# Early weight loads, freed slots and other DMA queues in an attention and GLU kernel

## Chip, cores and metric

The kernel runs on one core of a Trainium2 chip. The metric is the time of one execution on the device in microseconds (us), as the median of several runs. Profiles show one execution; their times count from the span's start. Engines are named as in the profile: PE is TensorE, PEld its weight load, DVE VectorE, ACT ScalarE, POOL GpSimd, SP SyncE. A name with q (SPq, ACTq, POOLq) is the engine's part that issues DMAs.

## What is computed

A pre-norm transformer layer in float32 on x of 2048 rows by 576 columns:

```python
x = A_x
h = x + _A_ref(_layernorm(x), A_wqkv, A_wo)      # 32 heads of 18; 8 keys, 2 positions apart
h2 = h + _B_ref(_layernorm(h), B_w_gate, B_w_up, B_w_down)
# _A_ref: logits = q . k at pos - 2*w (w = 0..7), softmax, weighted v, times wo
# _B_ref: (sigmoid(x @ w_gate) * (x @ w_up)) @ w_down, inner width 4608
```

## The kernel before

Even and odd positions are independent in the attention, so the rows are cut into four blocks of 512: blocks 0 and 1 are the even ones, 2 and 3 the odd ones. A block is held as four tiles (j) of 128 rows. Float32 operands of a product are split into a rounded high part and the remainder: `split` (L103) is one copy on ACT that rounds and one subtraction on DVE; each product is then three matmuls (high by high, low by high, high by low). The 576 columns are four chunks of 128 and a rest of 64; `split_rest` (L107) packs the rest's high and low part into one chunk.

*First stage.* `load_x(b)` (L331) reads a block by four DMAs on SP. `ln1` (L338) normalizes it tile by tile: `ln_j` (L118) takes statistics on DVE, the power on POOL and, for block 0, the scale on DVE (L134) and a copy of the rest columns (L135); PE transposes the tile (L139, L143) and `split` makes th and tl from it. `raw_w` and `qkv_w` (L355, L365) load and split the weights of a group of eight heads; `qkv` (L377) projects a block for one group and stores q, k and v to DRAM. `att_all` (L399) is a generator of attention steps, nearly all DVE work, that is stepped between projections. Blocks 0 and 1 come first; `front` (L478) multiplies block 0's attention output by wo, adds x, normalizes again and makes the first operands X of the GLU; it stores the transposed result to DRAM from a tile of the tag tok (L505, x<-tok in the profile). Near the end item 0's GLU weights are loaded into a slot of the tag tl (L538) and split by `first_split` (L507) into a slot of the tag th.

*Second stage.* The pools of the first stage are closed and their memory is used for new ones (gw, gh, gd, gc, st). Each new tile waits for the last users of the bytes under it. The 4608 inner columns are 36 chunks. An item is one chunk for one pair of blocks: kind std for one block (28 matmuls of 512 columns, `single` L644) or pair for two blocks with seven products instead of eight (`pair` L673). Items 0 to 13 are std for block 0, 14 to 35 are pair for blocks 0 and 1, then the same for blocks 2 and 3. For each item `load_gu` (L563) loads the weights into one of two buffers wg on SP, and `weights` (L575) splits them into w1 (two buffers), w2, w3, w4 and d; this is done one item ahead. Item 1's load goes out on POOL instead (L979), and item 0's down weights are split into a d tile of the new pool (L980, L981). The down product runs a pair of chunks behind (`down_tile`, L714, dp in the profile).

*Under the items* runs a second thread (`under_first` L888, `under_rest` L907), stepped by `bg_step` between matmul groups: the rest of block 1's attention, then `proj_scr` (L818), which does for block 1 what `front` did for block 0, and `operands`, which makes what pair items need. During the later items the same is done for blocks 2 and 3. `proj_scr` reads the attention output back from DRAM (`load_j` with i = 0, oj in the profile), the split wo half (wow), and x (`load_j` with i = 1, hj). All these loads are `paced` (L568): issued on SP behind the newest weight load.

*Order.* A scheduler puts every engine's instructions in one fixed order when the program is built: by trace order, moved forward by `tc.high_priority(n)` (HI is 400, HC 700), each as soon as it thinks the operands ready. `tc.issue_after(i)` puts instructions of the same engine behind i in that order, without a wait. On the chip each engine, and each DMA-issuing queue, works through its order and waits at its head.

Of the kernel before, what the change touches and what calls it, by code (L numbers as in the profile page):

```python
# [21 lines left out]
P = 128  # L22
# [38 lines left out]
def kernel(ctx, tc, x, wqkv, wo, wmlp, out):  # L61
# [36 lines left out]
    def f32(ap):  # L98
        return ap.bitcast(F32)
# [1 line left out]
    splits = []  # L101

    def split(hi, lo, src):  # L103
        act.activation(hi, src, AF.Copy)  # L104
        splits.append(dve.tensor_tensor(lo, src, f32(hi), ALU.subtract))  # L105

    def split_rest(t, src):  # L107
        act.activation(t, src, AF.Copy)
# [9 lines left out]
    def ln_j(xj, xn, on_act):  # L118
        bs = sm.tile([P, 2, 6], F32, bufs=4, name="bs")
        mv = sm.tile([P, 2], F32, bufs=4, name="mv")  # L120
        rstd = sm.tile([P, 1], F32, bufs=4, name="rstd")
        for k in range(2):
            dve.bn_stats(bs[:, k], xj[:, k * DH2:(k + 1) * DH2])
        dve.bn_aggr(mv, bs)
        dve.tensor_scalar(rstd, mv[:, 1:2], EPS, None, ALU.add)
        pool.tensor_tensor(rstd, rstd, mhalf, ALU.pow)
        if on_act:
            nm = sm.tile([P, 1], F32, bufs=4, name="nm")
            dve.tensor_scalar(nm, mv[:, 0:1], -1.0, None, ALU.mult)
            act.activation(xn[:, :D], xj, AF.Identity, bias=nm)  # L130
            act.activation(xn[:, :D], xn[:, :D], AF.Copy, scale=rstd)
            act.activation(xn[:, D:DX], xn[:, DM:D], AF.Copy)
        else:
            dve.tensor_scalar(xn[:, :D], xj, mv[:, 0:1], rstd, ALU.subtract, ALU.mult)  # L134
            dve.tensor_copy(xn[:, D:DX], xn[:, DM:D])  # L135

    def tr_main(ps, xn):
        for c in range(4):
# [86 lines left out]
    def step(gen, n):  # L225
        for _ in range(n):
            if next(gen, END) is END:
                return

    def drain(gen):  # L230
        for _ in gen:
            pass

    def run(*gens):
        live = list(gens)
        while live:
            live = [gn for gn in live if next(gn, END) is not END]
# [90 lines left out]
    def ev_tile(shape):  # L328
        return sar.tile(shape, F32, tag="ev", bufs=2, name="ev")

    def load_x(b):  # L331
        e, hf = BLOCKS[b]
        t = sah.tile([P, NS, D], F32, bufs=2, name="h")
        for j in range(NS):
            sp.dma_start(t[:, j], xv[e, hf][:, j])
        return t

    def ln1(b, xb):  # L338
        th = th3_tile(F32R) if b == 3 else th_tile()
        tl = tl_tile()  # L340
        yield th, tl
        xn = tok_tile()
        for j in range(NS):
            js = slice(j * P, (j + 1) * P)
            pri = 2 * HI if b == 0 else HI if b > 1 else 0
            with tc.high_priority(pri):
                ln_j(xb[:, j], xn[:, j], b > 1)
            pv = tr_main(mm_tile(), xn[:, j])
            pr = tr_rest(acc_tile(), xn[:, j])
            with tc.high_priority(pri):  # L350
                split(th[:, 0:4, js], tl[:, :, js], pv)
                split_rest(th[:, 4, js], pr)
            yield

    def raw_w(g):  # L355
        if g == 3:
            wr = sah.tile([P, NS, D], F32, bufs=2, name="h").rearrange("p j d -> p (j d)")
            wr = wr[:, :QC].rearrange("p (c n) -> p c n", c=5)
        else:
            wr = swo.tile([P, 5, NQ], F32, tag="wo", name="wr")  # L360
        for c in range(5):
            sp.dma_start(wr[:, c], wqkv[g][:, c * NQ:(c + 1) * NQ])
        return wr

    def qkv_w(g, wr=None):  # L365
        w = saw.tile([P, 2, 5, NQ], F32R, tag="qw", bufs=2, name="qw")
        for c in range(5):
            if wr is None:
                ws = sas.tile([P, NQ], F32, tag="wst", bufs=3, name="ws")
                sp.dma_start(ws, wqkv[g][:, c * NQ:(c + 1) * NQ])  # L370
            else:
                ws = wr[:, c]
            with tc.high_priority(3 * HI if g == 0 else HI):
                split(w[:, 0, c], w[:, 1, c], ws)
        return w

    def qkv(b, g, T, w):  # L377
        e, hf = BLOCKS[b]
        ev = ev_tile([P, 3, NS, CG])
        for j in range(NS):  # L380
            ps = acc_tile()
            passes.append(tok_major(ps, NQ, *T, slice(j * P, (j + 1) * P), w[:, 0], w[:, 1]))
            with tc.high_priority(HI):
                act.activation(ev[:, :, j], ps[:, :NQ].rearrange("p (t c) -> p t c", t=3), AF.Copy)  # L384
            yield
        r0 = LP + hf * TB
        with tc.high_priority(HI):
            act.dma_start(qscr[b][g], ev[:, 0].rearrange("p j c -> p (j c)"))
            for t, s in ((1, kscr), (2, vscr)):
# [173 lines left out]
    def load_gu(f, eng=sp, n=WC):  # L563
        ws = gw.tile([P, WC], F32, bufs=2, name="wg")
        behind[0] = eng.dma_start(ws[:, :n], wmlp[f][:, :n])
        return ws

    def paced(dst, src):  # L568
        with tc.issue_after(getattr(behind[0], "ins", behind[0])):
            behind[0] = sp.dma_start(dst, src)  # L570

    def d_tile():
        return gd.tile([P, 2, D], F32R, bufs=4, name="d")
# [235 lines left out]
            paced(f32(ww[a]), wscr[1][:, a])  # L809
        return tuple(ww)  # L810

    def load_j(pj, b, j, i):
        e, hf = BLOCKS[b]
        t = pj.tile([P, D if i else DX], F32, bufs=NS, name="hj" if i else "oj")
        paced(t, (xv[e, hf] if i else oscr[b])[:, j])
        return t

    def proj_scr(pj, b, raw, wos, ins=None, after=None):  # L818
        e, hf = BLOCKS[b]
        th, tl = th_tile(), tl_tile()  # L820

        def tile_j(t, j):
            js = slice(j * P, (j + 1) * P)

            def put(pv, cs):
                if cs.start == 0:
                    if b < 2:
                        pool.dma_start(hacc[b][:, j], t[1])
                    else:
                        rows = slice(0, 7, 6) if b == 2 else slice(2, 5, 2)  # L830
                        pool.dma_start(hsev[:, j // 2, rows, j % 2],
                                       t[1].rearrange("p (i n) -> p i n", i=2))
                act.activation(raw[:, cs, js], pv, AF.Copy)

            yield from proj_j(bg_bank, t, wos, th[:, :, js], tl[:, :, js], lambda: t[0], put, (1, 0))

        todo = []
        if ins is None:
            ins = []
            for j in range(NS):  # L840
# [24 lines left out]
        if b == 1:  # L865
            act.dma_start(xscr[b], raw[:, 0:2])
        return nxt
# [242 lines left out]
    for c, (kind, p, f) in enumerate(items):  # L1110
# [11 lines left out]
        if c == NF + NSTD:  # L1122
# [105 lines left out]
```

## Time and profile before

| | |
|---|---|
| median of 3 runs | 1590.44 us (1589.95 to 1590.81) |
| span of the profiled execution | 1589.2 us |
| PE, DVE, ACT, POOL busy | 98%, 80%, 55%, 12% |
| granted TensorE clock, mean | 0.993 |
| HBM read and written | 145.88 MB, 128.52 MB |

The profiled execution has no time of its own beside its span. In a group or timeline row stand the line, engine and operation, written and read tile, shapes, and in brackets how long the engine was idle before it and what ended that. A wait row reads: waiter, what it waited for, us in total, times, longest. The chain of waits is followed back from the last instruction. A busy PE can be a slow one: the granted clock is given with the windows.

### The profile page before, as it was taken

How to read it: one execution, taken by the hardware profiler on the slowest of the kernel's cores; microseconds unless marked ns; L12 is line 12 of the kernel's file. 1: busy time of each engine (PE TensorE's matmuls, PEld its weight loads, DVE VectorE, ACT ScalarE, POOL GpSimd, SP SyncE). 2: the span in 40 equal slices, each digit the busy share in tenths (PEclk: the TensorE clock that was granted, in tenths of full speed). 3: DMA queues.
4: the chain of work that ended last, by engine and by line, in shares of the span. 5: the costliest groups of instructions: out<-in, count | busy, mean ns of one | idle time of the engine just before them, and what ended most of it. 6: DMA issues, size and time to landing. Idle time of an engine off the chain costs nothing.

```text
span 1589.2 us, 22383 instructions
## 1 busy us (share of the span) xinstructions
PE 1553.3 (98%) x8532; PEld 1381.6 (87%) x8532; DVE 1268.1 (80%) x1931; ACT 869.2 (55%) x1546; POOL 184.2 (12%) x230
## 2 busy tenths in 40 slices
PE   7999979999999999999989999999999999999998
PEld 6999968888888888888879988888888888888887
DVE  7999988959999999999546687876677776677755
ACT  4432234425555666656443255776677776677761
POOL 1000000011010001000101100122112112212210
PEclk9999999999999999999999999999999999999999
DMA  7664544346367565665764234899989999989983
GB/s 267 208 206 163 193 184 165 133 177 246 104 164 205 157 170 139 166 191 149 210 203 143 100 110 110 182 186 181 176 169 183 184 173 180 177 170 182 184 170 124
DMA packets 76892, 273.50 MB, mean 172 GB/s; under 512 B 8336, under 2 KB 14224, under 8 KB 75888
## 3 DMA queue, kind: packets, MB, share of 16 engines
q0 software_dynamic: 27792, 105.89, 36.3%
q1 hardware_dynamic: 41360, 146.06, 27.4%
q10 hardware_dynamic: 7632, 20.12, 3.3%
q8 instruction: 67, 1.10, 0.3%
q14 instruction: 41, 0.34, 0.1%
HBM read 145.88 MB, written 128.52 MB: 173 GB/s over the span
## 4 chain that ended last, share of the span: by engine, by line
PE 55%; issue 27%; POOL 7%; DVE 6%; DMA 4%; ACT 1%; SPq 0%; POOLq 0%; ACTq 0%; DVEq 0%
PE b L609 23%; PE dp L723 15%; POOL h L794 7%; PE acc L150 6%; PE b L616 4%; PE b L150 1%; PE bgp L150 1%; DMA wg<-in_wmlp_dram 1%; DVE pr L182 1%; DMA x<-tok 1%; DVE pr L208 1%; DVE lg L186 1%; PE acc L152 1%; DMA tail<-h 1%; PE acc L153 1%
## 5 line engine op out<-in xcount | busy, mean ns | idle before, releaser
L609 PE MATMUL b<-tl,w 128*128 128x512 f32 x1716 | 438.1, 395 | 9.1 <-ACT w L104 6.5
L609 PEld LDWEIGHTS b<-tl,w 128*128 128x128 f32 x1716 | 311.7, 189 | 66.5 <-ACT w L104 7.7
L609 PE MATMUL b<-th,w 128*128 128x512 f32 x1368 | 352.8, 393 | 0.4 <-DVE s L698 0.3
L609 PEld LDWEIGHTS b<-th,w 128*128 128x128 f32 x1368 | 249.8, 188 | 46.7 <-DVE s L698 0.7
L104 ACT ACTIVATE w<-wg 128x640 fp32r<-128x640 f32 (+2 forms) x197 | 117.0, 598 | 125.2 <-PE b L616 59.8
L791 ACT ACTIVATE ev<-dp 128x576 f32<-128x576 f32 x224 | 145.0, 647 | 61.8 <-PE dp L785 58.2
L616 PE MATMUL b<-th,w 128*128 128x512 f32 x572 | 177.0, 391 | 0.0
L794 POOL DMA_DIRECT2D h<-ev x128 | 110.2, 862 | 456.8 <-ACT ev L791 440.5
L105 DVE TENSOR_TENSOR w<-wg,w 128x640 fp32r<-128x640 f32 (+2 forms) x197 | 126.8, 649 | 38.7 <-ACT w L104 38.3
L150 PE MATMUL acc<-qw,th 128*128 128x432 f32 x512 | 155.7, 365 | 1.2 <-DVE th L109 0.9
L105 DVE TENSOR_TENSOR w<-tw,w 128x512 fp32r<-128x512 f32 x116 | 79.6, 687 | 81.1 <-ACT w L104 80.2
L616 PEld LDWEIGHTS b<-th,w 128*128 128x128 f32 x572 | 107.7, 188 | 23.1
L723 PE MATMUL dp<-d,h0h 128*128 128x288 f32 x640 | 119.0, 296 | 1.7 <-DVE tail L733 1.7
L723 PE MATMUL dp<-d,h1h 128*128 128x288 f32 x640 | 120.0, 297 | 0.0
L723 PEld LDWEIGHTS dp<-d,h0h 128*128 128x128 f32 x640 | 99.4, 189 | 5.5 <-DVE tail L733 2.0
L150 PEld LDWEIGHTS acc<-qw,th 128*128 128x128 f32 x512 | 97.2, 190 | 6.5 <-DVE th L109 1.1
L723 PEld LDWEIGHTS dp<-d,h1h 128*128 128x128 f32 x640 | 99.5, 190 | 2.9
L731 ACT ACTIVATE stage<-dp 128x576 f32<-128x576 f32 x96 | 61.7, 646 | 62.4 <-PE dp L723 62.3
L104 ACT ACTIVATE w<-tw 128x512 fp32r<-128x512 f32 x116 | 72.8, 628 | 41.3 <-PE b L609 40.9
L150 PE MATMUL acc<-qw,tl 128*128 128x432 f32 x256 | 92.8, 362 | 0.0
L384 ACT ACTIVATE ev<-acc 128x432 f32<-128x432 f32 x64 | 33.9, 531 | 104.4 <-PE acc L153 97.7
L182 DVE TENSOR_TENSOR pr<-kw,q 128x2304 f32<-128x2304 f32 x32 | 81.7, 2552 | 2.8 <-DMA kw<-k 2.6
(278 smaller groups left out, 2899.8 us busy)
## 6 DMA issues: line engine op xcount, KB each, us to landing
h<-ev POOLq DMA_DIRECT2D x96, 576.0 KB, 7.2
wg<-in_wmlp_dram SPq DMA_DIRECT2D x49, 928.0 KB, 5.2
h<-stage POOLq DMA_DIRECT2D x24, 1152.0 KB, 10.6
wg<-in_wmlp_dram SPq DMA_DIRECT2D x36, 640.0 KB, 4.1
kw<-k SPq DMA_DIRECT2D x16, 792.0 KB, 4.4
vw<-v SPq DMA_DIRECT2D x16, 792.0 KB, 5.5
wd<-in_wmlp_dram SPq DMA_DIRECT2D x18, 576.0 KB, 7.2
h<-ev POOLq DMA_DIRECT2D x32, 288.0 KB, 6.8
```

The source lines that it names most:

```text
L104: act.activation(hi, src, AF.Copy)
L105: splits.append(dve.tensor_tensor(lo, src, f32(hi), ALU.subtract))
L150: pe.matmul(ps[:, :n], a[:, c, js], m[:, c], start=k == 0, stop=False)
L152: pe.matmul(ps[:, :n], th[:, 4, js], wh[:, 4], start=False, stop=False)
L182: dve.tensor_tensor(pr, both(kw, u), q[:, us].unsqueeze(2).broadcast_to([P, 2, W, CG]), ALU.mult)
L384: act.activation(ev[:, :, j], ps[:, :NQ].rearrange("p (t c) -> p t c", t=3), AF.Copy)
L609: pe.matmul(ps, wt[:, a, k0 + c], xx[:, m + c], start=first and k == 0, stop=k == 5, skip_group_check=True)
L616: pe.matmul(ps, wt[:, a, k0], xx[:, 4], start=False, stop=a == 1, skip_group_check=True)
L723: pe.matmul(ps[:, i, :DH2], a[:, js], d[:, m, i * DH2:(i + 1) * DH2], start=k == 0, stop=k == n)
L731: act.activation(hv, ps, AF.Copy)
L791: act.activation(hs[:, k % 2], ps[:, :, :DH2], AF.Copy)
L794: pool.dma_start(hsev[:, u, k0:k + 1], hs[:, :k + 1 - k0], accum_op=ALU.add, max_dma_last_dim=8 * D)
```

## The change

At the start, row tile 0 of block 0 is loaded first, then the first group's weights, then the other three tiles. The norm of tile 0 gets a higher priority. The norm of tile 1 is put behind the end of tile 0's norm on DVE, those of tiles 2 and 3 behind tile 0's split. The weight splits of the first group are put behind tile 0's norm (chunk 0) or split (chunks 1 to 4), those of the second group behind tile 0's split.

At the step to the GLU, item 1's weights are read on SP into the slot of the tag h in the first stage's pool, under the priority HI, after the projection of block 1 for the last group. Both first items' down weights and item 1's gate and up weights are split into slots of the tags tl and th, which live through both stages. The block that loaded item 1 on POOL and split item 0's down weights into a d tile is gone.

In `proj_scr`, block 1's oj loads go out on POOL and block 2's oj, wow and hj loads on ACT, neither paced. Block 1's wow and hj stay paced on SP, and so do block 3's loads.

```diff
@@ split
-        act.activation(hi, src, AF.Copy)
+        first = act.activation(hi, src, AF.Copy)
         splits.append(dve.tensor_tensor(lo, src, f32(hi), ALU.subtract))
+        return first, splits[-1]
@@ ln1
+            pri = (2 if j else 4) * HI if b == 0 else HI if b > 1 else 0
+            with ExitStack() as way:
+                way.enter_context(tc.high_priority(pri))
+                if b == 0 and j:
+                    way.enter_context(behind_all(done[j - 1:j] if j == 1 else cut[0][1:]))
+                done.append(ln_j(xb[:, j], xn[:, j], b > 1))
...
+                cut[j:] = [split(th[:, 0:4, js], tl[:, :, js], pv)]
@@ qkv_w
-            with tc.high_priority(3 * HI if g == 0 else HI):
+            with tc.high_priority(3 * HI if g == 0 else HI), behind_all(ties[c]):
@@ first stage
-    xb = load_x(0)
-    w = [qkv_w(0, raw_w(0))]
-    gl = ln1(0, xb)
+    xb = load_x(0, (0,))
+    wr = raw_w(0)
+    load_x(0, range(1, NS), xb)
+    normed, cut = [], []
+    gl = ln1(0, xb, normed, cut)
     T.append(next(gl))
-    run(gl, qkv(0, 0, T[0], w[0]))
-    w.append(qkv_w(1))
+    next(gl)
+    w = [qkv_w(0, wr, [normed[:1]] + [cut[0][1:]] * 2 + [cut[0]] * 2)]
+    call = qkv(0, 0, T[0], w[0])
+    next(call)
+    run(gl, call)
+    w.append(qkv_w(1, None, [cut[0]] * 5))
...
+    with tc.high_priority(HI):
+        wg1 = sah.tile([P, NS, D], F32, bufs=2, name="h").rearrange("p j d -> p (j d)")[:, :WC]
+        sp.dma_start(wg1, wmlp[1])
...
+    def first_down(ws):
+        d = xt.tile([P, 2, D], F32R, tag="tl", bufs=4, name="df")
+        split(d[:, 0], d[:, 1], ws[:, GU:WC])
+        return d
+
+    with tc.high_priority(HI):
+        wc = ww, first_down(wg)
+        wc_next = first_split(wg1), first_down(wg1)
@@ load_j, proj_scr
+        if eng is None:
+            paced(t, src)
+        else:
+            eng.dma_start(t, src)
...
-                ins.append([load_j(pj, b, j, 0), None])
+                ins.append([load_j(pj, b, j, 0, pool if b == 1 else act), None])
...
-            paced(f32(ww), wscr[0])
+            if b == 1:
+                paced(f32(ww), wscr[0])
+            else:
+                act.dma_start(f32(ww), wscr[0])
...
-                    ins[j][1] = load_j(pj, b, j, 1)
+                    ins[j][1] = load_j(pj, b, j, 1, None if b == 1 else act)
@@ items
-    with tc.high_priority(2 * HI):
-        wg2 = load_gu(1, pool)
-        d = d_tile()
-        split(d[:, 0], d[:, 1], wg[:, GU:WC])
-        wc = ww, d
-    wg = wg2
...
-        if c + 1 < len(items):
+        if c == 0:
+            wc = wc_next
+        elif c + 1 < len(items):
             wc = weights(items[c + 1][0], wg, c + 1 < NF + NSTD)
```

`behind_all(ties)` enters `tc.issue_after` for each instruction in ties.

More of the change, by code (lines that the diff above doesn't have):

```diff
@@ L134, in ln_j @@
             dve.tensor_scalar(xn[:, :D], xj, mv[:, 0:1], rstd, ALU.subtract, ALU.mult)
-            dve.tensor_copy(xn[:, D:DX], xn[:, DM:D])
+            return dve.tensor_copy(xn[:, D:DX], xn[:, DM:D])
     def tr_main(ps, xn):
@@ L329, in ev_tile, with behind_all, load_x, ln1 @@
         return sar.tile(shape, F32, tag="ev", bufs=2, name="ev")
-    def load_x(b):
+    def behind_all(ties):
+        way = ExitStack()
+        for i in ties:
+            way.enter_context(tc.issue_after(getattr(i, "ins", i)))
+        return way
+    def load_x(b, js=range(NS), t=None):
         e, hf = BLOCKS[b]
-        t = sah.tile([P, NS, D], F32, bufs=2, name="h")
-        for j in range(NS):
+        if t is None:
+            t = sah.tile([P, NS, D], F32, bufs=2, name="h")
+        for j in js:
             sp.dma_start(t[:, j], xv[e, hf][:, j])
         return t
-    def ln1(b, xb):
+    def ln1(b, xb, done=None, cut=None):
+        done = [] if done is None else done
+        cut = [] if cut is None else cut
         th = th3_tile(F32R) if b == 3 else th_tile()
@@ L344, in ln1 @@
             js = slice(j * P, (j + 1) * P)
-            pri = 2 * HI if b == 0 else HI if b > 1 else 0
-            with tc.high_priority(pri):
-                ln_j(xb[:, j], xn[:, j], b > 1)
+            pri = (2 if j else 4) * HI if b == 0 else HI if b > 1 else 0
[4 more added lines that the diff above has]
+                done.append(ln_j(xb[:, j], xn[:, j], b > 1))
             pv = tr_main(mm_tile(), xn[:, j])
@@ L350, in ln1 @@
             with tc.high_priority(pri):
-                split(th[:, 0:4, js], tl[:, :, js], pv)
+                cut[j:] = [split(th[:, 0:4, js], tl[:, :, js], pv)]
                 split_rest(th[:, 4, js], pr)
@@ L363, in raw_w, with qkv_w @@
         return wr
-    def qkv_w(g, wr=None):
+    def qkv_w(g, wr=None, ties=((),) * 5):
         w = saw.tile([P, 2, 5, NQ], F32R, tag="qw", bufs=2, name="qw")
@@ L810, in wos_early, with load_j @@
         return tuple(ww)
-    def load_j(pj, b, j, i):
+    def load_j(pj, b, j, i, eng=None):
         e, hf = BLOCKS[b]
         t = pj.tile([P, D if i else DX], F32, bufs=NS, name="hj" if i else "oj")
-        paced(t, (xv[e, hf] if i else oscr[b])[:, j])
+        src = (xv[e, hf] if i else oscr[b])[:, j]
+        if eng is None:
+            paced(t, src)
+        else:
+            eng.dma_start(t, src)
         return t
```

## Prediction

> **What bounds the kernel now.** I read the page first, then TensorE's waits stretch by stretch, then the windows around them.
>
> ```profile
> span 1589.2 us, 22383 instructions
> PE 1553.3 (98%) x8532; PEld 1381.6 (87%) x8532; DVE 1268.1 (80%) x1931; ACT 869.2 (55%) x1546; POOL 184.2 (12%) x230
> ```
>
> TensorE is busy for 98% of the span, so 35.9 us idle, and slow matmuls around the idle stretches, are all that an edit of order can win. The waits of PE are few:
>
> ```profile
> PE mm L139 <- DVE tok L134: 9.1, 1, 9.1
> PE acc L143 <- DVE tok L135: 1.6, 1, 1.6
> PE b L609 <- ACT w L104: 6.5, 1, 6.5
> PE b L609 <- DVE s L629: 2.5, 1, 2.5
> PE b L139 <- DMA oj<-o: 2.4, 1, 2.4
> PE bgp L139 <- DVE tl L105: 3.8, 1, 3.8
> ```
>
> (Waiter, what it waited for: us in total, times, longest.) In order: the start, the step from attention to the GLU, the first projection under the GLU (block 1), the second (block 2). The change touches exactly these four. The windows show the granted clock (the number after the last bracket) falling with the waits:
>
> ```profile
> 229.50:236.00 6.50, 0.01 (x1) 0.00 (x0) 2.92 (x2) 3.32 (x5) 0.00 (x0) 0.72 0.93 375
> 236.00:249.00 13.00, 10.46 (x30) 8.01 (x31) 9.09 (x13) 5.45 (x10) 0.00 (x0) 0.62 0.22 73
> 249.00:311.00 62.00, 61.84 (x331) 53.45 (x330) 61.40 (x75) 30.20 (x50) 0.71 (x1) 1.00 0.43 152
> 320.00:331.00 11.00, 11.00 (x63) 9.66 (x62) 4.85 (x10) 3.84 (x9) 0.00 (x0) 0.84 0.96 382
> 817.90:830.00 12.10, 8.04 (x38) 7.05 (x39) 7.12 (x13) 7.13 (x15) 0.00 (x0) 0.86 0.64 251
> ```
>
> (Columns: stretch, length, busy PE, PEld, DVE, ACT, POOL, clock, DMA share, GB/s.) From 249 to 311 both PE (61.84 of 62) and DVE (61.40) are full; that matters below.
>
> **Part A, the start.** Today all four rows of block 0 are loaded before the first weights, and VectorE takes statistics of other rows before it normalizes the first.
>
> ```profile
> 0.74 1.82 SPq L335 DMA_DIRECT2D h<-in_x_dram  x4
> 2.61 2.34 SPq L362 DMA_DIRECT2D wr<-in_wqkv_dram  x5
> 3.72 0.82 DVE L123 BATCH_NORM_STATS2 bs<-h 128x6 f32<-128x288 f32 x2 [3.72 <-DMA h<-in_x_dram]
> 5.32 0.56 POOL L126 TENSOR_TENSOR rstd<-rstd,mhalf 128x1 f32<-128x1 f32 x1 [3.88 <-DVE rstd L125]
> 8.45 0.57 DVE L134 TENSOR_SCALAR tok<-h,mv,rstd 128x576 f32<-128x576 f32 x1
> 9.07 1.11 PE L139 MATMUL mm<-ident,tok 128*128 128x128 f32 x4 [9.07 <-DVE tok L134]
> 8.93 2.68 DVE L105 TENSOR_TENSOR qw<-wr,qw 128x432 fp32r<-128x432 f32 x5
> 11.91 0.71 PE L150 MATMUL acc<-qw,th 128*128 128x432 f32 x1
> ```
>
> With the first row alone, the path from 3.72 is statistics 0.82, aggregate and add some 0.35, the power on POOL 0.56, the scale 0.57, with hand-overs about 0.3: 6.3. Transposes at 6.3 instead of 9.07 save 2.8. The next step saves more: today the rest columns (L135) stand behind five weight subtractions of 2.68; after the ties only the first stands there, so the first projection matmul could come near 8.1 (transposes to 7.4, the split's ACT half 0.6) instead of 11.91: 3.8. The weights do not hold it: three row loads (3 x 0.45 of issue, 0.86 MB) leave their way. What can eat it: rows 1 to 3 now arrive behind the weights, and their norms and the remaining subtractions (about 8.5 us of DVE) run beside only 5 us of matmuls for row 0. Bounds -3.8 and 0; I take **-2.5**, near the transposes' row.
>
> **Part B, attention to GLU.**
>
> ```profile
> ACT d L104 <- DMA x<-tok: 8.7, 1, 8.7
> 221.19 11.15 DMA x<-tok
> 220.41 30.68 SPq L565 DMA_DIRECT2D wg<-in_wmlp_dram  x3
> wg<-in_wmlp_dram SPq DMA_DIRECT2D x1, 928.0 KB, 11.7
> 234.36 0.60 ACT L653 ACTIVATE s<-b 128x512 f32<-128x512 f32 x1
> 236.03 1.22 PE L609 MATMUL b<-tl,w 128*128 128x512 f32 x2 [6.52 <-ACT w L104]
> 248.97 2.72 PE b L609 x12
> 251.69 0.45 PE b L616 x2
> DVE d L105 <- ACT d L104: 4.3, 1, 4.3
> DVE w L105 <- ACT w L104: 2.9, 1, 2.9
> ```
>
> ACT's split of item 0's down weights writes memory that the store of the transposed h (x<-tok) is still reading until 232.34. Queued behind it on ACT are item 0's sigmoid (234.36) and item 1's splits, for which PE stands. PE ends item 0 at 229.5 and has done item 1 at 248.97. One item is 28 matmuls, at 2.72/12 and 0.45/2 each: 6.4 us, with one down matmul 6.5. So 19.5 minus 6.5 = 13.0 us are lost: 6.5 + 2.5 of waits and 4.0 by the clock of 0.62. The change puts d of items 0 and 1 and all of item 1's weights into slots of the first pool (th, tl), and item 1's load, which POOL issued at 224.78, into an idle x buffer early in SP's order. None then depends on x<-tok. The moved work, three ACT and DVE pairs for w and two for d, about 3.3 us of DVE, goes ahead of 223; DVE is full there too, so attention steps slip by as much and nothing is won or lost. SP's extra 0.93 MB load shares the DMA around 180 to 190 with the wo loads: at most its own transfer, 2.5 us, on work with slack; counted in the residue.
>
> Bounds: -13.0 if nothing new stands in front of the sigmoid, -2.5 if it does (rival 1). The first is what the wait rows say about items 0 and 1; I leave 2 for it and take **-11.0**.
>
> **Part E, VectorE's debt.** DVE's idle in 222 to 250 is 4.3 + 2.9 + 0.9 = 8.1, and it is full from there to 311. PE comes 11 earlier, attention of block 1 at most 8.1 earlier, less as the items' own DVE work goes first. The scheduler can place items before the projection, so PE need not stand, but the operands that the first pair item (item 14) needs from block 1 get later against PE.
>
> ```profile
> 387.58 0.69 DVE L109 TENSOR_TENSOR th<-rd,th 64x512 fp32r<-64x512 f32 x1
> 388.65 1.52 PE L609 MATMUL b<-tl,w 128*128 128x512 f32 x6
> ```
>
> The last operand is ready at 388.3 and the pair item begins at 388.65; that operand is used in its seventh product, six products of 6 matmuls and three rests of 2 later, 9.6 us. This slack is about the 11 that PE gains, so bounds 0 and +8; I take **+0.5**.
>
> **Part C, projection of block 1.**
>
> ```profile
> 311.86 4.66 DMA o<-kw
> 316.65 1.75 SPq L570 DMA_DIRECT2D oj<-o  x4
> 338.90 0.56 POOL L828 DMA_DIRECT2D h<-hj  x1 [26.22 <-DVE hj L255]
> ```
>
> Four oj loads move from SP to POOL. They still wait for the store's landing (316.5). POOL takes 0.56 or more for each issue against 0.44, and wow (1.44 MB) is no longer behind them in one queue, so it shares the engines with them. First load later by 0.5 to 4, and PE comes earlier relative to it. The wait costs 2.4 plus 11.0 x 0.16 = 1.8 of clock now; bounds -2 and +6, taken **+2.0**.
>
> The Trainium skill (TensorE: Matmul & The Clock Gate, "Part 1: The HAM clock gate") lets the clock fall after an idle window of about 3.4 us; by that this 2.4 us wait would keep it and C would be near +0.5. The 0.84 behind that wait says otherwise, so the row is used.
>
> **Part D, projection of block 2.**
>
> ```profile
> 764.84 0.76 DVE L219 TENSOR_TENSOR kw<-kw 128x576 f32<-128x576 f32 x1
> 784.72 0.87 SPq L570 DMA_DIRECT2D oj<-o  x2
> 808.14 10.98 DMA wg<-in_wmlp_dram
> wow<-wo SPq DMA_DIRECT2D x1, 1440.0 KB, 14.1
> ```
>
> Here a weight load takes 10.98, because wow and three hj loads go out right behind it; ACT stands for it and PE for ACT: 3.8 + 0.3 of waits and 8.04 x 0.14 = 1.1 of clock, 5.2 in all. Nine loads go to ACT, unpaced: they cost ACT nine issues of some 0.4 us, and can start when the attention's memory is free, after 765, where SP's pacing held the first until 784.72. Then 808 is clear. Bounds -5.2 and +17.4 (rival 3); taken **-4.0**.
>
> **Sum.** -2.5 - 11.0 + 0.5 + 2.0 - 4.0 = -15.0. The profiled execution's span is 1589.2; the runs' median 1590.44 lies 1.24 above it, taken as unchanged. 1590.44 - 15.0 = **1575.4**.
>
> **Rivals.**
>
> 1. *ACT still stands at the step to the GLU.* Item 2's weights now need no wait for w4 and w2 (item 1 doesn't use them), so the compile-time order may put its splits before item 0's sigmoid. Its load took 11.7 (landing 232.1), its d still waits for x<-tok (232.34). Then the sigmoid comes again near 234 and PE restarts as today; B is between -2.5 and -6, say -4. Against it: the sigmoid has the highest priority (HC), and its matmuls end half an item, 3.2, before 229.5. Sum -8.0: 1582.4.
> 2. *The projection loads collide anyway.* Issued at the same time from ACT, wow loses its place behind wg and shares from the start; D is 0, C +3. Sum -2.5 - 11.0 + 0.5 + 3.0 = -10.0: 1580.4. For it: the 14.1 of wow; against: the twenty microseconds between 765 and the first paced load. The Trainium skill (DMA: Bandwidth & Descriptors, "Issuing engines are not separate DMA queues") says that issuing from several engines saves only issue time, as all run on the same 16 engines; the slow wow agrees.
> 3. *Slower: ACT pays for waiting in its queue.* The loads reach ACT's order as soon as the scheduler thinks the attention's memory free, just after 765, while the real store of o has yet to land (4.66 at block 1; more beside accumulating stores). ACT stands some 7 us with sigmoids and splits behind it, and the burst of 3.9 MB makes the next two weight loads late as the one at 808 is now: 7 + 2 x 5.2 = 17.4 lost there instead of 4.0 won. Sum -2.5 - 11.0 + 0.5 + 2.0 + 17.4 = +6.4: 1596.8. For it: nine issues with waits on an engine that PE needs every few microseconds. Against: ACT is 55% busy and two weight buffers lie between it and PE. It decides once stand and late loads cost over 14.2 (the other terms' 11.0 and 3.2 more).
> 4. *B is given back.* Item 14 waits for operands: E is +8 instead of 0.5. Sum -7.5: 1582.9.
>
> **How the numbers follow.** Forecast 0.50, rival 1 0.18, rival 2 0.10, rival 3 0.10, rival 4 0.07; 0.05 for no change that can be told (within 0.2%, 3.2 us, about what a measurement of this kernel can tell). Faster 0.85, same 0.05, slower 0.10. The range starts at all good ends but C: -3.8 - 13.0 - 5.2 + 0 - 1 = -23, 1567.4, and reaches over rivals 1, 2 and 4 with some margin to 1587; outside are rival 3, no change and a small tail below.
>
> **What would show it.** A: first transposes before 7, the first projection matmul before 9.5. B: no PE wait of over 1 us between 222 and 250 and clock 1.00 throughout; wrong if ACT waits for wg or x<-tok with the sigmoid behind it. C: the wait for oj no shorter than 2.4. D: no slow wg load before the block 2 transposes, and wow issued well before them; rival 3 if ACT shows a DMA-issue wait near 765. E: attention of block 1 ends less than 8 us earlier than now, less part A. If the span falls by less than 5, B or D has failed.

## The result: slower by 0.6%

The changed kernel takes 1599.12 us (median of 4 runs, 1597.95 to 1604.39) against 1590.62 of the kernel before on the same chip (4 runs, 1589.95 to 1592.30): a ratio of 1.0059, 95% interval 1.0040 to 1.0077. The forecast was 1575.4. The profiled execution took 1597.95; its page begins:

```profile
span 1596.2 us, 22385 instructions
PE 1553.4 (97%) x8532; PEld 1380.2 (86%) x8532; DVE 1268.1 (79%) x1931; ACT 868.8 (54%) x1546; POOL 186.1 (12%) x233
```

PE's work is unchanged (1553.3 before), so the 7.0 us more of span is idle PE. PE's waits after the change:

```profile
PE dp L754 <- ACT stage L762: 7.6, 1, 7.6
PE b L140 <- DMA oj<-o: 6.9, 1, 6.9
PE mm L140 <- DVE tok L135: 6.8, 2, 6.4
PE b L640 <- DVE s L660: 4.6, 2, 4.4
PE bgp L140 <- DVE tl L105: 1.4, 1, 1.4
```

The wait for ACT's w at the step to the GLU (6.5) is gone, and a wait for VectorE's s of 4.4 stands there (it was 2.5). The wait for oj grew from 2.4 to 6.9. The stall at block 2's first transposes shrank from 3.8 to 1.4, and a new one of 7.6, at a down product, stands ahead of it. The windows around the three places:

```profile
222.00:250.00 28.00, 23.41 (x102) 19.14 (x103) 26.93 (x31) 14.08 (x25) 0.76 (x1) 0.94 0.50 186
310.00:330.00 20.00, 13.10 (x70) 10.98 (x69) 7.60 (x14) 6.54 (x14) 2.18 (x4) 0.83 0.68 254
790.00:800.00 10.00, 6.22 (x37) 5.30 (x35) 0.00 (x0) 0.47 (x1) 0.00 (x0) 0.92 1.04 310
800.00:810.00 10.00, 6.18 (x23) 5.56 (x24) 2.32 (x4) 3.18 (x6) 0.00 (x0) 0.57 0.44 121
```

**Where the time went.** An item has one "hidden" multiply on VectorE for each of its blocks (s<-s,b in std items; most of the last pair items have none), 80 in all, in the same order in every kernel here. The start of the n-th in one kernel minus its start in the kernel before tells how far ahead (negative) or behind a kernel is at that point. The table has seven of the 80; times in the head are those of the kernel before. Each column of steps brackets one part: A and the first half of B lie ahead of 238.9, the rest of B up to 306.5, block 1's projection (C) between 306.5 and 389.5, block 2's loads and projection (D) between 770.6 and 841.7.

| kernel | 238.9 | 306.5 | 389.5 | 770.6 | 795.8 | 841.7 | 1513.4 |
|---|---|---|---|---|---|---|---|
| changed | -0.8 | -5.2 | -0.6 | +0.5 | +9.2 | +6.5 | +6.4 |
| e1_b2_sp | -0.6 | -4.9 | -0.1 | -0.2 | -0.2 | +0.2 | +0.1 |
| e2_b1_sp | -0.2 | -4.6 | -7.0 | -6.3 | +2.8 | +1.2 | +1.1 |
| e3_both_sp | +0.1 | -4.2 | -4.9 | -4.0 | -4.0 | -4.5 | -4.6 |
| e4_old_start | -2.5 | -6.4 | -7.1 | -7.3 | -7.3 | -6.8 | -6.6 |
| e5_oj_wow_act | -2.9 | -7.3 | -8.0 | -8.2 | -1.5 | -4.1 | -4.1 |
| e6_hj_act | -2.8 | -6.9 | -7.2 | -7.4 | -7.4 | -7.1 | -7.3 |
| e7_held | -9.2 | -12.7 | -12.9 | -13.0 | -13.1 | -13.4 | -13.5 |
| e8_rows_first | -0.8 | -5.2 | -7.7 | -7.8 | -7.8 | -7.7 | -7.8 |
| e9_after_held | -6.2 | -11.6 | -3.4 | -1.8 | +7.0 | +6.1 | +6.0 |
| e10_wow_halves | -10.3 | -15.3 | -14.5 | -14.7 | -14.7 | -15.5 | -15.6 |
| e11_wow_behind | -2.9 | -7.3 | -2.4 | -2.3 | -2.3 | -1.8 | -1.9 |
| e12_halves_hj_act | -9.6 | -13.5 | -13.4 | -13.0 | -11.5 | -12.0 | -11.9 |
| e13_b1_oj_act | -1.0 | -5.3 | -0.4 | -0.5 | -0.5 | -0.4 | -0.4 |

Each line is one execution. The programs of e4, e5, e6, e11 and e13 are the same up to 238.9 and lie between -2.9 and -1.0 there, so a difference of one microsecond between two lines says little.

So the changed kernel is 5.2 ahead before block 1's projection, loses nearly all of it there (-5.2 to -0.6), and loses 8.7 more at one place near 790. Of that it gets 2.7 back by 841.7, where the kernel before has its own stall.

*The start.* The first matmuls come as forecast:

```profile
6.35 1.11 PE L140 MATMUL mm<-ident,tok 128*128 128x128 f32 x4 [6.35 <-DVE tok L135]
8.15 0.73 PE L151 MATMUL acc<-qw,th 128*128 128x432 f32 x1 [0.47 <-ACT th L104]
```

They were at 9.07 and 11.91. VectorE pays for it: in the first 12 us it is busy 6.4 instead of 7.5. Its longest waits of the first 60 us for x and for POOL's power are:

```profile
DVE bs L124 <- DMA h<-in_x_dram: 4.6, 2, 3.7
DVE tok L135 <- POOL rstd L127: 2.7, 6, 0.8
```

In the kernel before they were 4.4 and 1.1 in all, and the 3.7 for the first row is there too.

*The step to the GLU.* Timelines of the changed kernel, first ACT and PE, then VectorE. PE waits from 234.45 to 238.83 for the multiply of L660:

```profile
229.92 0.60 ACT L684 ACTIVATE s<-b 128x512 f32<-128x512 f32 x1
...
230.66 0.62 PE L647 MATMUL b<-th,wf 128*128 128x512 f32 x2
...
238.83 2.93 PE L640 MATMUL b<-tl,wf 128*128 128x512 f32 x6 [4.38 <-DVE s L660]
```

```profile
229.44 2.55 DVE L187 TENSOR_REDUCE lg<-pr 128x128 f32<-128x2304 f32 x1
231.91 0.55 DVE L105 TENSOR_TENSOR wf<-h,wf 128x384 fp32r<-128x384 f32 x1
232.37 2.55 DVE L183 TENSOR_TENSOR pr<-kw,q 128x2304 f32<-128x2304 f32 x1
234.84 0.75 DVE L105 TENSOR_TENSOR df<-h,df 128x576 fp32r<-128x576 f32 x1
235.51 2.54 DVE L187 TENSOR_REDUCE lg<-pr 128x128 f32<-128x2304 f32 x1
238.08 0.69 DVE L660 TENSOR_TENSOR s<-s,b 128x512 f32<-128x512 f32 x1
```

No bracket in VectorE's rows: it waits for nothing. The sigmoid of item 0 is done at 230.5 and its last matmul at 231.3, so the multiply could run. Three attention operations of 2.55 and two weight subtractions stand in VectorE's order from 229.44 on, ahead of it, and item 1 needs the bank that the multiply reads.

*Block 2's loads.* ACT's issues in the changed kernel and its wait for the weight load that SP issues at 786.01, and that load:

```profile
769.78 0.33 ACTq L850 DMA_DIRECT2D oj<-o  x1
...
777.20 0.33 ACTq L883 DMA_DIRECT2D wow<-wo  x1
785.31 0.37 ACTq L850 DMA_DIRECT2D hj<-in_x_dram  x1
786.91 1.35 ACTq L850 DMA_DIRECT2D hj<-in_x_dram  x3
802.50 0.74 ACT L104 ACTIVATE w<-wg 128x640 fp32r<-128x640 f32 x1 [12.02 <-DMA wg<-in_wmlp_dram]
...
wg<-in_wmlp_dram SPq DMA_DIRECT2D x1, 928.0 KB, 16.5
```

(Last row: the DMA issues of 780 to 805, with us to landing.) The queues of that stretch, with packets, MB and their share of the 16 engines' time:

```profile
q0 software_dynamic: 544, 2.36, 46.9%
q1 hardware_dynamic: 471, 2.60, 26.6%
q10 hardware_dynamic: 710, 2.64, 26.3%
```

SP's queue, with the weights, is q1; ACT's, new here, is q10; POOL's accumulating stores are q0. SP's queue had a quarter of the engines' time, and the weight load had to share even that with two loads of wo (tl<-wo, 0.72 MB each, issued from 776.64 on, landed at 790.0 and 796.3). ACT stood 12.0 for the weights; its copy of stage, for which PE stood 7.6, is behind that split in its order. The same stretch of the kernel before has no q10:

```profile
q0 software_dynamic: 542, 2.35, 46.8%
q1 hardware_dynamic: 671, 2.83, 31.0%
```

### The profile page after: what moved, and what is told of

The parts are those of the page before. It is cut to its first block, busy times and chain, and to the rows that moved or that the text cites. A ratio compares the mean times of both kernels' runs of the same rounds, so it can differ in the third digit from the quotient of the medians.

```text
span 1596.2 us, 22385 instructions
## 1 busy us (share of the span) xinstructions
PE 1553.4 (97%) x8532; PEld 1380.2 (86%) x8532; DVE 1268.1 (79%) x1931; ACT 868.8 (54%) x1546; POOL 186.1 (12%) x233
## 4 chain that ended last, share of the span: by engine, by line
PE 56%; issue 14%; DMA 4%; POOL 3%; DVE 3%; ACT 1%; POOLq 0%; SPq 0%; DVEq 0%; ACTq 0%
PE b L640 29%; PE dp L754 13%; PE dp L816 6%; PE b L647 5%; POOL h L825 3%; DMA wg<-in_wmlp_dram 2%; PE b L151 1%; PE bgp L151 1%; PE b L140 0%; DMA tail<-h 0%; DVE w L105 0%; DMA h<-ev 0%; DMA oj<-o 0%; DVE s L660 0%; DVE pr L209 0%
## 5 line engine op out<-in xcount | busy, mean ns | idle before, releaser
L640 PE MATMUL b<-th,w 128*128 128x512 f32 x1356 | 348.5, 392 | 1.0 <-DVE s L729 0.9
L640 PEld LDWEIGHTS b<-th,w 128*128 128x128 f32 x1356 | 246.6, 188 | 46.4 <-DVE s L729 1.3
L104 ACT ACTIVATE w<-wg 128x384 fp32r<-128x384 f32 (+2 forms) x194 | 115.1, 598 | 127.9 <-PE b L647 61.4
L647 PE MATMUL b<-th,w 128*128 128x512 f32 x568 | 175.4, 390 | 0.0
L105 DVE TENSOR_TENSOR w<-wg,w 128x384 fp32r<-128x384 f32 (+2 forms) x194 | 124.8, 650 | 38.9 <-ACT w L104 38.6
L647 PEld LDWEIGHTS b<-th,w 128*128 128x128 f32 x568 | 106.7, 188 | 22.9
L754 PE MATMUL dp<-d,h0h 128*128 128x288 f32 x608 | 112.5, 295 | 0.8 <-DVE tail L764 0.8
L754 PEld LDWEIGHTS dp<-d,h0h 128*128 128x128 f32 x608 | 94.2, 189 | 4.2 <-DVE tail L764 1.1
## 6 DMA issues: line engine op xcount, KB each, us to landing
h<-stage POOLq DMA_DIRECT2D x24, 1152.0 KB, 10.8
```

The lines of the kernel that those rows point to most:

```text
L104: first = act.activation(hi, src, AF.Copy)
L640: pe.matmul(ps, wt[:, a, k0 + c], xx[:, m + c], start=first and k == 0, stop=k == 5, skip_group_check=True)
L647: pe.matmul(ps, wt[:, a, k0], xx[:, 4], start=False, stop=a == 1, skip_group_check=True)
L754: pe.matmul(ps[:, i, :DH2], a[:, js], d[:, m, i * DH2:(i + 1) * DH2], start=k == 0, stop=k == n)
```

## The experiments

Ratios are to the kernel before, run beside each; the brackets hold the 95% interval. The changed kernel's own interval (1.0040 to 1.0077) makes a difference to it uncertain by about 3 us either way; the leads of the table stand beside such differences as a second measure.

| run | ratio |
|---|---|
| e1_b2_sp | 1.0015 [1.0005, 1.0025] |
| e2_b1_sp | 1.0034 [1.0021, 1.0048] |
| e3_both_sp | 0.9970 [0.9958, 0.9983] |
| e4_old_start | 0.9959 [0.9945, 0.9972] |
| e5_oj_wow_act | 0.9993 [0.9982, 1.0003] |
| e6_hj_act | 0.9945 [0.9932, 0.9959] |
| e7_held | 0.9920 [0.9908, 0.9933] |
| e8_rows_first | 0.9962 [0.9949, 0.9974] |
| e9_after_held | 1.0041 [1.0027, 1.0055] |
| e10_wow_halves | 0.9915 [0.9901, 0.9928] |
| e11_wow_behind | 1.0011 [1.0002, 1.0020] |
| e12_halves_hj_act | 0.9939 [0.9926, 0.9953] |
| e13_b1_oj_act | 1.0003 [0.9994, 1.0012] |

### Taking back the queues and the start

**e1_b2_sp**

```diff
-                ins.append([load_j(pj, b, j, 0, pool if b == 1 else act), None])
+                ins.append([load_j(pj, b, j, 0, pool if b == 1 else None), None])
...
-            if b == 1:
-                paced(f32(ww), wscr[0])
-            else:
-                act.dma_start(f32(ww), wscr[0])
+            paced(f32(ww), wscr[0])
...
-                    ins[j][1] = load_j(pj, b, j, 1, None if b == 1 else act)
+                    ins[j][1] = load_j(pj, b, j, 1)
```

> The changed kernel with block 2's nine projection loads (oj, wow, hj) back on SP, paced; all else as changed. Theory (the burst on ACT's queue made one weight load take 16.4 us and costs PE 9.2 at 796 to 805, against 4.0 of the old stall): the lag to before stays near +0.5 at 795 and near +0.5 to +1.5 behind block 2's projection, so the time is 6 to 8 below the changed kernel's, 1591 to 1593. Rival (PE waits there because it runs at a different point against the attention, wherever the loads are issued): the 9 us stay, 1597 to 1600.

1590.92, 0.0044 of the ratio below the changed kernel, 7.0 us (6.2 by the leads at 1513.4). At 795.8 it is at -0.2: the 9 us near 790 are block 2's loads on ACT.

**e2_b1_sp**

```diff
-                ins.append([load_j(pj, b, j, 0, pool if b == 1 else act), None])
+                ins.append([load_j(pj, b, j, 0, None if b == 1 else act), None])
```

> The changed kernel with block 1's four oj loads back on SP, paced; block 2's stay on ACT. Theory (on POOL they share the engines with wow and land 6.7 us after their issue, where SP's took 3.1; PE stands 6.9 instead of 2.4): wait for oj back to 2 to 4, the lead of 5 at 311 stays to about -4, and the end is 3.5 to 4.5 lower, 1594 to 1596. Rival (PE, being 5 earlier, stands longer for the same store however its rows are read back): the lead is eaten as before, 1598 to 1600.

1593.97, 4.0 below the changed kernel by the ratios (the intervals overlap a little) and 5.3 by the leads. The wait for oj is 2.0 and the lead even grows through block 1's projection (-4.6 to -7.0), where the kernel before has its own stall; it grows by less in e3, with the same loads, because there the clock fell (last section).

**e3_both_sp** has both edits.

> The changed kernel with all projection loads of both blocks back on SP, paced: the start and the step to the GLU alone are changed. Theory (the two queue changes cost about 4 and 6 to 7, and add): 1585 to 1588, faster than before. Rival (the lead of B is given back wherever the first projection's loads stand): 1590 to 1592.

1584.32, faster than before by 0.3%. Start and step to the GLU alone win; the two queue edits lost that and more. Undone together they give 14.1 by the ratios, where 7.0 and 4.0 add up to 11.0; within the uncertainty they add, and by the leads it is 11.0 against 6.2 and 5.3.

**e4_old_start** also undoes the start (`load_x(0)` whole and first, one priority, no ties).

> As e3_both_sp, and the start as before too (rows, weights, priorities and ties): only the step to the GLU is changed. Theory (the new start saves 3 at the first matmuls and loses all of it by 34 us, since rows 1 to 3 come later, and leaves VectorE's attention 0.7 to 1.8 late): 1 to 2 below e3_both_sp, 1584 to 1586. Rival (the start is worth the 2.5 forecast): 2 to 3 above it.

1581.91. The intervals of e3 and e4 overlap (medians' ratios differ by 0.0011, 1.7 us): the times show no gain of the new start and do not prove a loss. The traces show a lag at 238.9, before anything else differs. There e4 is 2.6 ahead of e3, and the five kernels with the old start and the new step (e4, e5, e6, e11, e13: -2.9 to -1.0) are on the mean 2.0 ahead of the five with the new start's ties (changed, e1, e2, e3, e8: -0.8 to +0.1). Windows of 0 to 12 us, e3_both_sp first, then e4_old_start (columns as in the prediction: PE, PEld, DVE, ...):

```profile
0.00:12.00 12.00, 4.03 (x12) 3.04 (x13) 6.22 (x17) 6.09 (x11) 2.19 (x12) 1.00 0.85 289
```

```profile
0.00:12.00 12.00, 1.91 (x7) 1.30 (x8) 8.15 (x25) 5.77 (x11) 3.39 (x14) 1.00 0.87 305
```

The new start gives PE 2.1 more busy time and VectorE 1.9 less. VectorE's last operation ahead of the attention then ends at 35.4 in e3 and at 33.2 in e4. The first attention multiply waits for a load of k and is no good mark (36.1 to 38.2 in the kernels with the new start, 35.6 to 37.8 with the old). The second one shows the lag, e3 first, then e4:

```profile
53.45 2.56 DVE L183 TENSOR_TENSOR pr<-kw,q 128x2304 f32<-128x2304 f32 x1
```

```profile
51.55 2.56 DVE L183 TENSOR_TENSOR pr<-kw,q 128x2304 f32<-128x2304 f32 x1
```

The lag is still 1.95 at the multiply near 161. PE's gain does not last that long, as it then waits for VectorE's splits (22.88 busy in e3 from 12 to 36, 23.97 in e4); VectorE's lag does, and at item 0 the hidden multiply stands behind the attention in VectorE's order. So up to item 0 VectorE's work counts. That the lag is also lost at the end is not shown.

**e8_rows_first** is e3_both_sp with

```diff
-    xb = load_x(0, (0,))
+    xb = load_x(0)
     wr = raw_w(0)
-    load_x(0, range(1, NS), xb)
```

> As e3_both_sp (new start, new step, old queues), but all four rows are loaded ahead of the first weights, as before; priorities and ties stay new. If the late rows make the new start lose (VectorE is idle 4.8 for rows of x and does 1.8 less in the first 12 us): the first attention multiply comes at 35.5 to 36.5 instead of 37.85, and the time is at or below e4_old_start, 2 to 4 below e3_both_sp. If the ties do, which hold back statistics that VectorE could make: it stays near 37.5 and the time within 1 of e3_both_sp.

The first attention multiply came at 37.14, between the two expectations, but by the spread above it decides nothing. At the later marks e8 stands with the new starts (second multiply at 52.55, -0.8 at 238.9), though all its rows are loaded first. So nothing shows that the late rows cost; the lag goes with ties and priorities, which are not divided. 1584.7 can't be told from e3 or e4. By the leads e8 ends no worse than e4 (-7.8 and -6.6): it gained 2.5 in block 1's projection, where its wait of 1.84 left the clock at 1.00.

### VectorE's order at item 0

**e7_held** is e4_old_start with

```diff
+    mult = [None]
     def hidden(sg, ps, name):
-        dve.tensor_tensor(sg, sg, ps, ALU.mult)
+        mult[0] = dve.tensor_tensor(sg, sg, ps, ALU.mult)
...
+    def held(i):
+        if i >= 4:
+            with tc.issue_after(getattr(mult[0], "ins", mult[0])):
+                for k in range(5) if i == 4 else (5,):
+                    twice(k)
...
-            hid = single(X, w, p, late, twice)
+            hid = single(X, w, p, late, twice if c else held)
```

> As e4_old_start, with the attention steps that are stepped under item 0 placed behind item 0's hidden multiply in VectorE's order, so that no attention operation of 2.55 stands between the sigmoid and it. Theory (VectorE is full from 222 to 311, so its backlog is only met at another place): the wait of 4.4 at item 1 goes to under 1, hidden 1 comes 5 to 7 earlier, but the wait for oj near 310 grows by 3 to 7 and the time is within 2.5 of e4_old_start. Rival (the wait was lost time, as the items can go on without the attention): the lead stays and the time is 5 to 7 lower.

1576.56: the rival was right. The stretch of the step, e4_old_start first, then e7_held:

```profile
222.00:250.00 28.00, 23.61 (x101) 19.55 (x100) 26.97 (x30) 13.40 (x21) 0.76 (x1) 0.88 0.51 184
```

```profile
222.00:250.00 28.00, 28.00 (x140) 24.04 (x139) 23.48 (x28) 13.17 (x23) 0.76 (x1) 1.00 0.66 244
```

PE is busy 28.00 of 28.00 at clock 1.00, VectorE even idles for 4.5, and the lead of 12.7 is never given back: the store of block 1's attention output comes 10.4 later than in e4 (315.29 against 304.85), but the items that PE does meanwhile need nothing of it. PE's waits for oj sum to 0.7.

**e9_after_held** puts the same edit into the changed kernel.

> The changed kernel whole, with only the attention steps stepped under item 0 placed behind item 0's hidden multiply on VectorE. If the moved wait is worth the same in the changed kernel as beside the old queues (e7_held: 5 to 7): hidden 1 comes about 7 earlier, and the time is 5 to 7 below the changed kernel's, 1591 to 1594. If the projection waits for its rows and for block 2's loads regardless: the lead is eaten at 310 and 790, and the time is within 2 of the changed kernel's 1599.

1596.05, 2.9 below the changed kernel by the ratios (their intervals overlap) and 0.4 by the leads. 5.4 to 6.4 are won until 306.5 and most is eaten at oj (wait 5.9, -11.6 to -3.4 and to -1.8). The order on VectorE and the queues have to be mended together.

### Which loads collide

**e5_oj_wow_act** and **e6_hj_act** are e4_old_start with oj and wow, or hj alone, of block 2 on ACT.

> As e4_old_start (only the step to the GLU changed), with block 2's oj and wow on ACT, unpaced, and hj on SP, paced. If hj (four loads issued right beside the weight load of 786) made that load late: it takes at most 10 us, PE stands under 2 for it, and the stall of 4.1 at the first transposes of block 2 shrinks to 1.4 as in the changed kernel, so 0 to 4 below e4_old_start. If wow's 1.44 MB did: the weight load takes 13 to 16 again, and the time is 4 to 8 above e4_old_start.

> As e4_old_start, with block 2's hj alone on ACT, unpaced; oj and wow paced on SP. If hj beside the weight load is the cause: that load takes over 10, and the time is 4 to 8 above e4_old_start. If wow is: no weight load before 800 over 8, the later one, which then shares with wow alone and not with hj, is 2 to 4 shorter than before, and the time is 0 to 3 below e4_old_start.

e5: 1588.1, 5.4 above e4 by the ratios. wow goes out at 768.59, with the last oj landing at 769.0, the weight load behind it at 777.40 and takes 14.4, and PE stands:

```profile
768.59 0.33 ACTq L875 DMA_DIRECT2D wow<-wo  x1
777.40 0.33 SPq L588 DMA_DIRECT2D wg<-in_wmlp_dram  x1
791.86 0.74 ACT L104 ACTIVATE w<-wg 128x640 fp32r<-128x640 f32 x1 [9.99 <-DMA wg<-in_wmlp_dram]
...
PE dp L746 <- ACT stage L754: 5.6, 1, 5.6
```

(ACT's, SP's and again ACT's timeline, then a wait row of PE.) e6: 1581.88, the same as e4 within the intervals. There hj goes out at 761.8 to 766.4 and lands 3.0 after its issue (median). So wow, beside loads and stores that the kernel before has there too, suffices to hold the weights up, and hj alone, issued earlier, does no harm. One expectation failed: the later weight load, with hj no longer beside it, was to be 2 to 4 shorter, but took 11.46 (10.98 before), and the stall at the transposes is still 4.3.

**e10_wow_halves** is e7_held with wow of block 2 in two paced halves, the first behind the second oj:

```diff
+                if b == 2 and j == 1:
+                    ww = pj.tile([P, 2, 5, DH2], F32R, name="wow")
+                    paced(f32(ww[:, 0]), wscr[0][:, 0])
...
+            else:
+                paced(f32(ww[:, 1]), wscr[0][:, 1])
```

> As e7_held, with block 2's wow loaded in two halves on SP, paced: one behind the second oj, one where the whole was. If the stall of 3.8 at block 2's first transposes comes from wow and three hj on top of the weight load beside them: that load takes 8 instead of 11, PE waits 1 to 2 there, and the time is 2 to 4 below e7_held, 1572 to 1575. If halving only moves the sharing to the weight load before: the same within 1.5, or up to 3 slower.

1575.28, the fastest, but not to be told from e7_held. Of its 2.1 of lead over e7, 1.1 is there at 238.9 already, before the edit's place. The stall is still 3.6, and the weight load beside the second half takes 10.8 (10.98 before).

**e12_halves_hj_act** adds hj on ACT.

> As e10_wow_halves, with block 2's hj on ACT, unpaced, as in e6_hj_act: beside the late weight load (10.8 in e10_wow_halves) now runs only half of wow, 0.72 MB, and two oj. If bytes beside that load are what makes it late: it takes 6 to 8, the stall of 3.6 at block 2's transposes goes under 1, its clock stays at 1.00, and the time is 3 to 5 below e10_wow_halves, 1570 to 1572.5. If something else holds it: the wait stays at 3 to 4 and the time within 1.

1579.01: a miss, and 3.8 above e10 by the ratios; of the 3.7 that it lies behind e10 by the leads, 1.6 is there at 770.6 already. The weight load of 796.62 still holds ACT until 807.23, 10.6, with only half of wow and two oj near it, and an earlier weight load now costs a stall of 1.6. Through the same time runs the accumulating store h<-stage, here the DMA view of 792 to 808:

```profile
q0 software_dynamic: 272, 1.18, 37.1%
...
h<-stage POOLq DMA_DIRECT2D x1, 1152.0 KB, 15.3
```

Its queue takes 37.1% of the engines' time in these 16 us for 1.18 MB. In the changed kernel a weight load issued at 818.62 with almost nothing but such a store beside it took 8.5, and the store's queue held 68.8% of the engines' time then. That the store is what mostly holds the weight load here is likely, but taking it away was not tried.

### Why oj is late on POOL

**e11_wow_behind** is e4_old_start with block 1's oj and then wow on POOL; **e13_b1_oj_act** has block 1's oj on ACT, wow and hj as in e4.

```diff
-            paced(f32(ww), wscr[0])
+            if b == 1:
+                pool.dma_start(f32(ww), wscr[0])
+            else:
+                paced(f32(ww), wscr[0])
```

> As e4_old_start, with block 1's oj on POOL as in the changed kernel, and block 1's wow on POOL too, behind them in the same queue. If oj landed late on POOL because wow, issued on SP 1.1 earlier, shared the engines (6.7 us against 3.1): oj takes 3 to 4 again, PE waits 2 to 3 for it, and the time is within 1.5 of e4_old_start. If loads issued by POOL are slow by themselves: oj takes 6 or more, PE waits 5 to 7, and the time is 3 to 5 above it.

> As e4_old_start, with block 1's four oj loads issued by ACT instead of SP; wow and hj stay on SP and so start as soon as the store has landed, as in the changed kernel. If wow beside them is what makes oj late there (6.7 in the changed kernel): oj takes 5 to 7 from its issue, PE waits 5 or more. If POOL's own issue and queue are: oj takes 3 to 4 as on SP, though ACT stands for the store with its splits behind, and PE waits 2 to 4.

e11: 1591.05, 8.3 above e4 by the ratios, and PE waits 6.3. The first oj took 3.94, as the theory of wow had it, but it landed 3.5 later than in e4. 1.3 of that is the store's landing: without wow ahead of them on SP, hj's loads went out at 303.51, just before the store of o, and the store took 7.0 instead of 4.8. 1.1 is POOL's issue, which came 1.2 behind the landing where SP's came 0.1 behind it, and 1.1 the longer load. e13: 1589.57, PE waits 5.6 and 2.0. The landing of the first oj, from the chain of waits, in the changed kernel (POOL, wow beside it), e13 (ACT, wow beside it), e11 (POOL, wow behind it) and e3_both_sp (SP, wow behind it):

```profile
312.67 6.74 DMA oj<-o
```

```profile
311.06 6.63 DMA oj<-o
```

```profile
312.78 3.94 DMA oj<-o
```

```profile
312.29 2.94 DMA oj<-o
```

With wow beside it oj takes 6.6 to 6.7 from POOL or ACT; with wow behind it 2.9 on SP and 3.9 on POOL. hj follows wow on SP, so the first two rows do not tell the two apart: the last oj loads of e13, issued at 318.90 and 319.26 with wow landed (318.24), still took 6.8 and 7.1 beside hj and a weight load. In the changed kernel wow goes out on SP at 311.57, as soon as the store has landed, and oj on POOL 1.1 later. The old order on one queue worked as a priority: oj first, wow and hj after. The Trainium skill (DMA: Bandwidth & Descriptors, "Issuing engines are not separate DMA queues") says that DMAs of all issuing engines run on the same 16 engines and interleave; 6.63 from ACT and 6.74 from POOL agree.

## Why the prediction was wrong

By the leads of the changed kernel, A, B and E together brought -5.2 (forecast -13.0), C +4.7 (+2.0), D +5.9 (-4.0), and 1.0 was lost at 611, which no term has: +6.4 in place of -15.0.

**A, -2.5: no gain.** The step that failed is the bound by the path of the first matmuls. Its times came true (6.35, 8.15), and the text named what could eat it, but took 0 as the worst end. From 36 to 222 VectorE is about as full as PE (177.8 and 182.6 busy of 186 in e4_old_start) and has the last word at item 0, where its 1.9 less of work in the first 12 us comes back as a lag of 2.0 (mean of five kernels against five). Whether this is a loss at the end stays open: the times of e3 and e4 differ by 1.7 with overlapping intervals.

**B, -11.0, with E, +0.5: the mechanism right, the place of the debt wrong.** No wait for x<-tok is left, and B's mechanism is as told. But in e4_old_start, where B stands alone, the lead at 306.5 is 6.4 instead of the 10.5 of B and E; it is 12.7 in e7_held. The step that failed is E's: it looked for VectorE's debt at item 14, 150 us later, and placed nothing at item 0. There it cost, in e4_old_start, 4.4 of wait and 2.7 of slow matmuls, as two sixes took 2.93 and 2.77 where a six takes 1.52:

```profile
230.85 1.52 PE L632 MATMUL b<-th,wf 128*128 128x512 f32 x6
...
237.21 2.93 PE L632 MATMUL b<-tl,wf 128*128 128x512 f32 x6 [4.39 <-DVE s L652]
239.94 2.77 PE L632 MATMUL b<-th,wf 128*128 128x512 f32 x6
```

e7_held, which only moves the attention steps behind that multiply, gains 6.3 at 306.5 and 6.2 in the ratio (0.9959 to 0.9920). The window 222 to 250, asked to be at clock 1.00 without a wait, was the right test and failed in the changed kernel (0.94) and held in e7 (1.00). The claim that attention of block 1 would end less than 8 earlier held (its store of o went out 5.2 earlier, 306.69 against 311.86) but is moot: it may end 10 later at no cost.

**C, +2.0: the sign right, the size too small.** The lead fell by 4.7 (-5.2 to -0.6). The mechanism was named, the sharing with wow and 0.5 to 4 for the late first load; the mis-sized term is this lateness. The load took 3.8 longer from its issue (6.74 against 2.94) and was issued 1.1 later, 4.9 in all.

**D, -4.0: wrong, and the largest error, +5.9 (+0.5 at 770.6 to +6.4 at the end).** The step that failed is "can start when the attention's memory is free, after 765 ... Then 808 is clear". Free memory does not issue a load: the second thread's steps do. oj went out from 769.8, wow at 777.2, hj at 785.3 to 788.3, beside the weight load of 786.0, which took 16.5. Its reading of the old stall is not borne out either: the load that took 10.98 "because wow and three hj loads go out right behind it" took 11.46 without hj (e6) and 10.6 with half of wow and no hj (e12). The stall at 817 did shrink (3.8 to 1.4), and this is the 2.7 that came back; 8.7 went for it.

**Rivals.** Rival 3 gave 1596.8, near the result, and its sum of +6.4 is the trace's, but by luck: it kept 13.0 of A, B and E, of which 5.2 came, and put 17.4 at block 2, where 5.9 was lost. It had half its mechanism: the burst made a weight load late, as it said, but ACT never stood for the store of o, and one late load of 16.5 did what two of 11 were to do. Rival 2's mechanism, the collision of loads, is what D and C both show, only dearer than its price of 0 and +3. Rival 1 did not occur: the sigmoid ran at 229.92 without a wait. Rival 4's debt came at item 0 instead of item 14. The 1.0 at 611 came with one weight load: ACT waited 1.57 for it before its split at 609.77, 0.44 at that place in the kernel before, and PE stood 0.7 at 616.85 for ACT. Why the load was late was not followed.

## What to carry to other kernels

A paced queue can also be an order of importance among transfers, as here: before a load is moved to a free queue, list what is in flight at the time it will really be issued, and which of these PE needs first. When a wait is removed, look on the engine that ends last next (here VectorE) at what its fixed order has ahead of the operation now awaited, at that very place. An earlier first matmul was worth nothing here, where VectorE had the last word at the end of the stage. Where executions of one program differ by a microsecond or two, compare several traces before a cause of that size is named.

## What was not expected of the hardware

Short waits can cost clock too, and their length alone does not decide. The first projection matmul of block 1 and a window of 5 us behind it, in e4_old_start and in e2_b1_sp (PE's timeline, then the window, with the granted clock behind the last bracket):

```profile
313.27 0.66 PE L140 MATMUL b<-ident,oj 128*128 128x128 f32 x4 [2.19 <-DMA oj<-o]
...
315.00:320.00 5.00, 5.00 (x24) 4.13 (x22) 2.77 (x5) 1.96 (x4) 0.00 (x0) 0.72 1.01 398
```

```profile
314.94 0.66 PE L140 MATMUL b<-ident,oj 128*128 128x128 f32 x4 [2.02 <-DMA oj<-o]
...
315.00:320.00 5.00, 5.00 (x33) 4.23 (x34) 2.94 (x5) 2.56 (x5) 0.00 (x0) 1.00 1.04 414
```

A wait of 2.19 brings the clock to 0.72, one of 2.02 leaves it at 1.00. Behind the start, every PE wait of 2.3 or more in these traces was followed by matmuls at a granted clock of 0.50, and none of 1.84 or less. In between, 1.93 (e3), 2.06 (e5) and 2.19 (e4) were, and 1.98 (e13), 2.02 and 2.18 (both e2) were not. The price shows from 306.5 to 389.5 in the table: where the clock stayed (e2, e8) the lead grew by 2.4 and 2.5, where it fell (e3, e4, e5, e6) by 0.3 to 0.7. The Trainium skill (TensorE: Matmul & The Clock Gate, "Part 1: The HAM clock gate") puts the return to half clock after an idle window of about 3.4 us; here it followed waits from 1.93 on.
